# Last batch, chunks two by two: seven products for eight in every second block of a and b

## The chip, the cores and the metric

The kernel runs on one core of one Trainium2 chip. The metric is device time of one execution in microseconds (us); the time before the change is the median of three runs. Engines are named as the profile names them: PE is TensorE (matmuls), PEld its weight loads, DVE is VectorE, ACT is ScalarE, POOL is GpSimd, SP is SyncE, which here only issues DMAs. Every engine works through its own instructions in order, and waits on semaphores for the others.

## The reference

Four batches, N = 5824 tokens, C = 256 channels, d_ff = 1024. A cross-covariance attention gives for each batch a 256 x 256 matrix, and a multiplicative feed-forward follows:

```python
qn = q / (norm(q, axis=1) + 1e-06); kn = k / (norm(k, axis=1) + 1e-06)
s = kn.transpose(0, 2, 1) @ qn / tau
a = softmax(s)                     # [B, 256, 256]
x = (v @ a).reshape(B * N, 256)
out = ((x @ w1) * (x @ w2) @ w3) @ w_out
```

## The kernel before, in words

**Folding.** Since v @ a @ w1 = v @ (a @ w1), the kernel folds the attention matrix into w1 and w2 once per batch: `Wf[n]` holds, for each half `ct` of the channels, a 128 x 1024 block for a (w = 0) and one for b (w = 1). `fold` (L439) runs eight PSUM tiles of 128 x 512 through `fold_mm` (L420); four of them are scaled by the softmax sums on ACT (L435) and four on DVE (L437). Likewise w3 @ w_out is one 1024 x 256 matrix `W_sb`. The folds of batch n run near the end of batch n - 1.

**Main loop.** The 5824 tokens of a batch are 11 chunks of 512 (c = 0 to 10) and one of 192 (c = 11). `emit_ab` (L651) is one slot: for chunk c and block j (128 of the 1024 hidden channels, j = 0 to 7) it issues two 128x512 matmuls into a PSUM tile for a, two for b (L657, one for each channel half `ct`), an ACT copy of a to SBUF as bf16 (L663) and the DVE product a*b (L676) into `abh`, which lies in the pool "big". The tiles for a and b rotate over four PSUM banks, ab0 to ab3. The other four banks are out0, out1, out2 and G.

**Seven products.** With all eight blocks of a chunk there, `seven_products` (L552) does (a*b) @ W_sb, as 2 x 2 blocks, in Strassen and Winograd's form: seven products of eight 128x128 matmuls (L570) in place of eight, in seven or eight groups. It needs four sums S1 to S4 of halves of `abh` (L589 and L592, 128x1024 bf16), made on POOL in batches 0 to 2 and on DVE in the last batch, and sums of W_sb (`comb_T`), made once. S2 is made from S1, S4 from S2. Four products go one after another through PSUM tile A, and after each an ACT copy `keep` (L580) takes the running sum out before the next may be added to it; B and C are joined by DVE adds (L583). In the last batch the sums stand inside the groups: S1 at once, S2 and p1, S3 and p5, p6, S4 and p7, p2, p4, p3. In the other batches each sum is issued two slots after the one before it. The last full chunk (c = 10) and the short one go through `emit_out` (L719).

**Order of the work.** It is written out by hand. For each slot the loop (L972) runs what an agenda holds for the modelled clock (loads, transposes, the softmax of the next batch), then `emit_ab`, then takes groups from `pend` as long as `room` (2, which is one group of a product or two of `emit_out`) lasts, then the sums that are due. So a typical slot is a, b and one product. A load is preceded by `gate` (L642), a one-element POOL copy that waits for the newest `abh` and so holds the DMA issue behind it (L120).

Of the kernel before, what the change touches and what calls it, by code (L numbers as in the profile page):

```python
# [9 lines left out]
AF = mybir.ActivationFunctionType  # L10
ALU = mybir.AluOpType
F32 = DT.float32
BF16 = DT.bfloat16

P = 128
# [3 lines left out]
LAG_FAST = 4  # L19
BIG_BUFS = 21  # L20
MM_COL = 1.0 / 2400.0
MM_FIX = 0.0025
# [3 lines left out]
def kernel(  # L26
# [12 lines left out]
    nc = tc.nc  # L39

    B, N, C = q.shape
    T, D = out.shape
    F = moe_w1.shape[1]
# [205 lines left out]
    S = {}  # L249
# [27 lines left out]
    def soft_units(n):  # L277
# [142 lines left out]
        def fold_mm(key, c2, tag="ab", on_act=True):  # L420

            w, c1, lo, hi = key
            if c2 == 0:
                turn = (lo // 512 * 4 + w * CT + c1) % 3
                home = bank(tag) if n == 0 or turn == 2 else {"tag": ("out2", "G")[turn], "bufs": 1}
                st[key] = psum.tile([P, 512], F32, name=f"fold_{n}_{w}_{c1}_{lo}", **home)
            m = st[key][:, : hi - lo]
            nc.tensor.matmul(  # L428
                m, lhsT=st["e"][:, c2, c1 * P : (c1 + 1) * P], rhs=w12[:, c2, w, lo:hi],
                start=(c2 == 0), stop=(c2 == CT - 1),  # L430
            )
            if c2 == CT - 1:
                dst = Wf[n][:, c1, w, lo:hi]
                if on_act:
                    nc.scalar.activation(out=dst, in_=m, func=AF.Copy, scale=st["rs"][:, c1 : c1 + 1])  # L435
                else:
                    nc.vector.tensor_scalar_mul(dst, m, st["rs"][:, c1 : c1 + 1])  # L437

        def fold(i, tag="ab"):  # L439
            h, rest = divmod(i, 4)  # L440
            w, c1 = divmod(rest, 2)
            for c2 in range(CT):
                fold_mm((w, c1, h * 512, (h + 1) * 512), c2, tag, i % 2 == 0 or (n == 0 and i == 7))

# [42 lines left out]
            + [(0.43, 16.5 + 1.1 * i, lambda i=i: fold(i)) for i in range(8)]  # L487
        )


    clock = [0.0]
    agenda = []

    def run_due(upto=None):
        lim = clock[0] if upto is None else upto
        while agenda and agenda[0][0] <= lim:
            _, _, cost, fn = agenda.pop(0)
            clock[0] += cost
            fn()
# [3 lines left out]
    def at(t, cost, fn):  # L503
        seq[0] += 1
        agenda.append((t, seq[0], cost, fn))
# [9 lines left out]
    def rhs_of(b, c, ct):  # L515
        vT, vTt = vTs[b]
        if c < NCH - 1:
            return vT[:, 4 * c : 4 * c + 4, ct, :]
        return vTt[:, ct, :]
# [32 lines left out]
    def seven_products(b, c, k1, k2):  # L552

        T = comb["T"]
        a11, a21 = k1[:, :, : 2 * P], k1[:, :, 2 * P :]
        a12, a22 = k2[:, :, : 2 * P], k2[:, :, 2 * P :]
        w1 = [W_sb[:, j, :P] for j in range(4)]
        w21 = [W_sb[:, 4 + j, :P] for j in range(4)]
        w22 = [W_sb[:, 4 + j, P:] for j in range(4)]
        t1, t2, t3, t4 = ([T[:, i, j, :] for j in range(4)] for i in range(4))  # L560
        st, sums = {}, {}
        tags = {"A": "out0", "B": "out1", "C": "out1" if b < B - 1 else "out2"}
        adder = nc.gpsimd if b < B - 1 else nc.vector

        def product(nm, a, w, first=False):
            if first:
                st[nm] = psum.tile([P, 2, P], F32, tag=tags[nm], name=f"prod{nm}_{b}_{c}", bufs=1)
            for j in range(4):
                for i in range(2):
                    nc.tensor.matmul(  # L570
                        st[nm][:, i, :], lhsT=a[:, j, i * P : (i + 1) * P], rhs=w[j],
                        start=(first and j == 0 and i == 0), stop=(j == 3), skip_group_check=True,
                    )
            clock[0] += 8 * (P * MM_COL + MM_FIX)

        def quarter(r, d):
            return st["o"][:, 2 * r : 2 * r + 2, d * P : (d + 1) * P]

        def keep(r, d):
            nc.scalar.copy(quarter(r, d), st["A"])  # L580

        def join(nm, r, d):
            nc.vector.tensor_add(quarter(r, d), st[nm], quarter(r, d))  # L583

        def operand(i):

            x = sums[i] = work.tile([P, 4, 2 * P], BF16, tag=f"S{i}", name=f"S{i}_{b}_{c}", bufs=1)
            if i == 1:
                adder.tensor_add(x, a21, a22)  # L589
            else:  # L590
                u, w = {2: (sums.get(1), a11), 3: (a11, a21), 4: (a12, sums.get(2))}[i]
                adder.tensor_sub(x, u, w)  # L592

        def p1():
            st["o"] = work.tile([P, 4, D], F32, tag="o_sb", name=f"osb_{b}_{c}", bufs=3)
            product("A", a11, w1, True)
            keep(0, 0)

        def p5():
            product("C", sums[1], t1, True)  # L600

        def p6():
            product("A", sums[2], t2)
            keep(0, 1)

        def p7():
            product("A", sums[3], t3)
            keep(1, 1)

        def p2():  # L610
            product("B", a12, w21, True)

        def p4():
            product("A", a22, t4)
            keep(1, 0)

        def p3():
            product("C", sums[4], w22)

        def store():  # L620
            rows = out[b * N : b * N + NT * P, :].rearrange("(p i) c -> p i c", i=NT)
            nc.sync.dma_start(out=rows[:, 4 * c : 4 * c + 4, :], in_=st["o"])

        def S(i):
            return lambda: operand(i)

        def J(*x):
            return lambda: join(*x)

        def then(fn):  # L630
            return lambda: following.append(fn)

        if b == B - 1:
            return [S(1)], [
                [S(2), p1], [S(3), p5], [p6], [S(4), p7], [J("C", 1, 1), p2],
                [J("B", 0, 0), p4], [p3, J("C", 0, 1), store],
            ]
        return [S(1), S(2), S(3), S(4)], [
            [p1], [p2, then(J("B", 0, 0))], [p6], [p5], [p7], [then(J("C", 1, 1))], [p4], [p3, then(J("C", 0, 1)), then(store)],
        ]  # L640
# [10 lines left out]
    def emit_ab(b, c, j):  # L651
# [27 lines left out]
        if not seven(b, c):  # L679
            if b == B - 1 or c == NCH - 1:  # L680
                lag = LAG if b == B - 1 else FT + LAG_FAST
                pend.append((slot[0] + lag, 1, lambda only=None: emit_out(b, c, j, ab, only)))
            elif j == FT - 1:
                for i in range(FT):
                    fn = lambda i=i, ab2=tuple(halves[c]): emit_half(b, c, i, ab2)
                    pend.append((slot[0] + 1 + LAG_FAST + i, 1, fn))
        elif j == FT - 1:
            sums, groups = seven_products(b, c, *halves[c])
            for i, fn in enumerate(sums):
                due_sums.append((slot[0] + 2 * i, fn))  # L690
            ready = slot[0] + 1 + (LAG_FAST if b < B - 1 else 0)
            for i, group in enumerate(groups):
                wait = 0 if b == B - 1 else i
                pend.append((ready + wait, 2, lambda group=group: [fn() for fn in group]))
        clock[0] += 4 * (n * MM_COL + MM_FIX)

    def emit_half(b, c, i, ab2):

# [212 lines left out]
    def make_agenda(b):  # L911
# [34 lines left out]
        if b == 0:  # L946
            for i in range(4):
                at(COMB + 2.6 * i, 0.0, lambda i=i: combine_weights(i))
        if n == B:
            agenda.sort()  # L950
            return
# [14 lines left out]

    for b in range(B):
        make_agenda(b)
        order = [(c, j) for c in range(NCH) for j in range(FT)]
        if b == 0:  # L970
            order[: 2 * FT] = [(c, h * 4 + j) for h in range(2) for c in range(2) for j in range(4)]
        for s, (c, j) in enumerate(order):  # L972
            run_due()
            while following:
                following.pop(0)()
            scores_due(s)
            emit_ab(b, c, j)
            lag = 0
            if b == B - 1 and c >= NCH - 2:
                lag = LAG_END if c == NCH - 1 else LAG + (LAG_END - LAG) * (j + 1) // FT  # L980
            room = 2
            while slot[0] > W_SLOT and len(pend) > lag and pend[0][0] <= slot[0] and pend[0][1] <= room:
                _, size, fn = pend.pop(0)
                fn()
                room -= size
                run_due()
            while due_sums and due_sums[0][0] <= slot[0]:
                due_sums.pop(0)[1]()
        run_due(1e9)
# [39 lines left out]
```

## Time and profile before

| What | Value |
|---|---|
| Time of the program, median of 3 runs | 555.21 us (555.05 to 555.32) |
| Span of the profiled execution, first to last instruction | 553.5 us |
| PE, DVE, ACT, POOL busy over the span | 542.1, 435.5, 375.8, 304.8 us |
| Last batch: from its first 128x512 matmul to its last | 431.8 to 541.2 us |
| PE busy from 441.75 to 541.20 us | 99.45 of 99.45 us |
| DVE, ACT, POOL busy in the same stretch | 86.33, 60.98, 2.94 us |
| One 128x512 bf16 sum on POOL | not in the program; 128x1024: 2.13 us |

The profile shows one execution, so sums of durations are to be set against its span of 553.5 us; the median of the runs is 1.7 us above it, which covers what lies outside the first and the last instruction. A recorded duration of a DVE or ACT instruction can overlap the next one a little, so the rate of an engine is read from the distance of starts. The recorded end of a matmul is modelled.

### The profile page before, as it was taken

To read this page: it belongs to the slowest core of one execution; us is meant where nothing else is said; L and a number is where in the kernel's file an instruction comes from. 1 tells how busy PE (TensorE), PEld (TensorE's weight loads), DVE (VectorE), ACT (ScalarE), POOL (GpSimd) and SP (SyncE) were. 2 spreads that over 40 slices of the span, in tenths; PEclk is the share of its full clock that TensorE was granted. 3 is DMA by queue.
4 is the path that set the end of the run, shared out by engine and by line. 5 is a ranking of instruction groups with operands and counts; after the bars stand their busy time and mean duration, and the time that the engine had idled before them with its cause. 6 is when DMAs were issued, how large, how long until landed. Compare 5 with 4: busy or idle time off the path is not lost.

```text
span 553.5 us, 12330 instructions
## 1 busy us (share of the span) xinstructions
PE 542.1 (98%) x4630; PEld 352.9 (64%) x4630; DVE 435.5 (79%) x789; ACT 375.8 (68%) x757; POOL 304.8 (55%) x257
## 2 busy tenths in 40 slices
PE   7799999999999999999999999999999999999997
PEld 4564577766666666666667566666666666666665
DVE  5567747899976787988876788888877688988984
ACT  5436647788866777777766777777766666566663
POOL 4150022678889678889887588898987400010000
PEclk9999999999999999999999999999999999999999
DMA  9999888975666879576554777875650245343102
GB/s 213 211 206 209 167 164 201 224 180 82 152 140 155 191 150 165 126 147 136 128 127 122 153 153 156 164 147 124 147 115 40 83 117 117 91 110 82 77 40 97
DMA packets 74972, 77.61 MB, mean 140 GB/s; under 512 B 54176, under 2 KB 58784, under 8 KB 74912
## 3 DMA queue, kind: packets, MB, share of 16 engines
q0 software_dynamic: 15616, 38.93, 40.3%
q1 hardware_dynamic: 58928, 37.17, 24.2%
q8 instruction: 36, 0.59, 0.4%
q10 hardware_dynamic: 368, 0.72, 0.3%
q14 instruction: 24, 0.20, 0.1%
HBM read 78.91 MB, written 23.86 MB: 186 GB/s over the span
## 4 chain that ended last, share of the span: by engine, by line
PE 93%; DMA 5%; DVE 0%; ACT 0%; POOL 0%; issue 0%; POOLq 0%
PE a L657 28%; PE b L657 28%; PE prodA L570 13%; PE prodC L570 6%; PE G L200 5%; PE prodB L570 3%; DMA k<-in_k_dram 3%; PE o L707 3%; PE fold L428 2%; DMA q<-in_q_dram 2%; PE o_out L738 2%; PE w L882 1%; PE G L271 0%; PE narrow L452 0%; PE sqq L259 0%
## 5 line engine op out<-in xcount | busy, mean ns | idle before, releaser
L676 DVE TENSOR_TENSOR abh<-as,b 128x512 bf16<-128x512 bf16 x352 | 240.0, 684 | 82.0 <-ACT as L663 76.2
L663 ACT CAST as<-a 128x512 bf16<-128x512 f32 (+1 forms) x384 | 215.4, 562 | 94.8 <-PE a L657 61.5
L657 PE MATMUL a<-vT,Wf 128*128 128x512 bf16 x704 | 209.4, 379 | 0.1
L657 PE MATMUL b<-vT,Wf 128*128 128x512 bf16 x704 | 209.4, 379 | 0.0
L657 PEld LDWEIGHTS <-Wf 128*128 128x128 bf16 x1536 | 141.1, 98 | 100.6 <-issue 0.8
L570 PEld LDWEIGHTS <-S 128*128 128x128 bf16 x1248 | 82.6, 98 | 34.3
L212 DVE TENSOR_TENSOR acc<-acc,sq 128x512 f32<-128x512 f32 x132 | 91.6, 694 | 3.0 <-ACT sq L197 1.9
L580 ACT COPY osb<-prodA 128x256 f32<-128x256 f32 x156 | 58.1, 372 | 42.0 <-PE prodA L570 41.4
L589 POOL TENSOR_TENSOR S<-abh,abh 128x1024 bf16<-128x1024 bf16 x29 | 61.7, 2127 | 32.1 <-DVE abh L676 16.6
L570 PEld LDWEIGHTS <-abh 128*128 128x128 bf16 x936 | 62.0, 98 | 25.7 <-issue 0.2
L592 POOL TENSOR_TENSOR S<-S,abh 128x1024 bf16<-128x1024 bf16 x29 | 61.8, 2131 | 1.9
L592 POOL TENSOR_TENSOR S<-abh 128x1024 bf16<-128x1024 bf16 x29 | 61.8, 2131 | 0.1
L592 POOL TENSOR_TENSOR S<-abh,S 128x1024 bf16<-128x1024 bf16 x29 | 61.7, 2129 | 0.1
L645 POOL COPY gate_t<-abh 1x1 bf16<-1x1 bf16 x39 | 7.2, 185 | 80.1 <-DVE abh L676 79.9
L570 PE MATMUL prodA<-comb_T,S 128*128 128x128 bf16 x624 | 47.6, 219 | 0.0
L200 PE MATMUL G<-k,q 128*128 128x256 bf16 x276 | 47.0, 273 | 0.0
L197 ACT ACTIVATE sq<-q 128x512 f32<-128x512 bf16 x69 | 43.8, 634 | 0.0
L197 ACT ACTIVATE sq<-k 128x512 f32<-128x512 bf16 x69 | 43.4, 628 | 0.0
L583 DVE TENSOR_TENSOR osb<-prodC,osb 128x256 f32<-128x256 f32 x78 | 32.5, 417 | 0.0
L200 PEld LDWEIGHTS <-q 128*128 128x128 bf16 x276 | 23.9, 98 | 3.6
L570 PE MATMUL prodB<-W_sb,abh 128*128 128x128 bf16 x312 | 23.8, 219 | 0.1
L570 PE MATMUL prodC<-comb_T,S 128*128 128x128 bf16 x312 | 23.8, 219 | 0.0
(139 smaller groups left out, 444.0 us busy)
## 6 DMA issues: line engine op xcount, KB each, us to landing
out_dram<-osb SPq DMA_DIRECT2D x44, 512.0 KB, 3.2
k<-in_k_dram POOLq DMA_DIRECT2D x19, 512.0 KB, 8.3
v<-in_v_dram POOLq DMA_DIRECT2D x19, 512.0 KB, 5.2
q<-in_q_dram POOLq DMA_DIRECT2D x18, 512.0 KB, 5.8
w_wout<-in_moe_w_dram POOLq DMA_DIRECT2D x1, 2048.0 KB, 21.6
k<-in_k_dram POOLq DMA_DIRECT2D x4, 320.0 KB, 6.5
v<-in_v_dram POOLq DMA_DIRECT2D x4, 320.0 KB, 5.4
q<-in_q_dram POOLq DMA_DIRECT2D x3, 320.0 KB, 5.2
```

The lines of the kernel that those rows point to most:

```text
L197: nc.scalar.activation(out=sqs[0][:, :, part, :], in_=src[:, o : o + 2, :], func=AF.Square)
L200: nc.tensor.matmul(G[:, ct, :], lhsT=qt[:, i, ct * P : (ct + 1) * P], rhs=kt[:, i, :], start=(pr == 0 and part == 0 and ct == 0), stop=(pr ...
L212: nc.vector.tensor_add(accs[n], accs[n], sqs[0][:, part - 2])
L570: nc.tensor.matmul(st[nm][:, i, :], lhsT=a[:, j, i * P : (i + 1) * P], rhs=w[j], start=(first and j == 0 and i == 0), stop=(j == 3), skip_ ...
L580: nc.scalar.copy(quarter(r, d), st["A"])
L583: nc.vector.tensor_add(quarter(r, d), st[nm], quarter(r, d))
L589: adder.tensor_add(x, a21, a22)
L592: adder.tensor_sub(x, u, w)
L657: nc.tensor.matmul(t[:, :n], lhsT=Wf[b][:, ct, w, j * P : (j + 1) * P], rhs=rhs_of(b, c, ct), start=(ct == 0), stop=(ct == CT - 1),)
L663: nc.scalar.copy(a_sb[:, :n], tiles[0][:, :n])
L676: nc.vector.tensor_mul(ab, a_sb, tiles[1])
L707: nc.tensor.matmul(t[:, k, :], lhsT=ab2[j // 4][:, j % 4, (2 * h + k) * P : (2 * h + k + 1) * P], rhs=W_sb[:, j, :], start=(j == 0 and k = ...
```

## The change

Only the work for batch 3, the last, is changed. Its chunks 0 to 7 go in pairs (0,1), (2,3), (4,5), (6,7). A pair has 16 slots, k = 0 to 3 with four steps `sub` each. Block 2k+1 of both chunks is done as before, with eight 128x512 matmuls (`plain`). Block 2k of both chunks is one 2 x 2 product, of the two channel halves of the weights of a and b with the two chunks' two channel halves, and is done with seven 128x512 matmuls in place of eight. For that:

- `weight_sums` makes four sums of the folded weights (128 x 1024 each, S[0] to S[3] in `wsums`) by eight `scalar_tensor_tensor` instructions on DVE that read the fold's PSUM tile; for this batch ACT scales all eight folds, and the folds of b come before those of a.
- `token_sum` makes four sums per pair of `v` transposed (128x512 bf16 each, T[0] to T[3] in `tsums`) on POOL, during the pair before.
- In `emit_pair` the partial sums lie in PSUM tiles X, Y, T and Z, which are read while they are still being added to: ACT copies X to Y (PSUM to PSUM) and T to SBUF (`t5`, float32); DVE adds X and `t5` into Z (PSUM) and into `b1` (bf16); then four DVE products write `abh`.
- The sums S1 to S4 of chunks 0 to 6 go back to POOL, those of chunk 7 stay on DVE, and both are issued two slots apart, as in the other batches. The products of both chunks of a pair start only after the pair's 16 slots, the second chunk's eight slots after the first's. From chunk 8 on `room` is 4: two product groups may go into one slot. Chunks 8 and 9 keep the sums inside the groups.

The core of the diff:

```diff
-                turn = (lo // 512 * 4 + w * CT + c1) % 3
+                turn = (lo // 512 * 4 + ((1 - w) if n in PAIRED else w) * CT + c1) % 3
...
-                if on_act:
+                if n in PAIRED:
+                    nc.scalar.activation(out=dst, in_=m, func=AF.Copy, scale=st["rs"][:, c1 : c1 + 1])
+                    weight_sums(w, c1, lo, hi, m)
...
+        def weight_sums(w, c1, lo, hi, m):
...
+            S = [wsums[n][x // 2][:, x % 2, lo:hi] for x in range(4)]
+            b1 = Wf[n][:, 0, 1, lo:hi]
+            todo = {
+                (1, 0): [], (1, 1): [(0, b1, ALU.add)], (0, 0): [(1, S[0], ALU.subtract), (2, b1, ALU.subtract)],
+                (0, 1): [(3, S[1], ALU.add)],
+            }
+            for x, other, op in todo[w, c1]:
+                nc.vector.scalar_tensor_tensor(
+                    out=S[x], in0=m, scalar=st["rs"][:, c1 : c1 + 1], in1=other, op0=ALU.mult, op1=op
...
+    def token_sum(b, c, i):
+        if i == 0:
+            tsums[b, c] = in_pool.tile([P, 4, 4, P], BF16, tag="big", name=f"tsum_{b}_{c}", bufs=BIG_BUFS)
+        t = tsums[b, c]
+        b11, b12, b21, b22 = (rhs_of(b, c + d, ct) for ct in range(CT) for d in range(2))
+        if i == 0:
+            nc.gpsimd.tensor_sub(t[:, 0], b12, b11)
+        elif i == 1:
+            nc.gpsimd.tensor_sub(t[:, 1], t[:, 0], b22)
+        elif i == 2:
+            nc.gpsimd.tensor_sub(t[:, 2], b22, b12)
+        else:
+            nc.gpsimd.tensor_add(t[:, 3], b21, t[:, 1])
...
+        late = b == B - 1 and c >= 2 + max(PAIRED[b])
-        adder = nc.gpsimd if b < B - 1 else nc.vector
+        adder = nc.vector if b == B - 1 and c > max(PAIRED[b]) else nc.gpsimd
...
+    def queue_products(b, c, delay=0):
+        sums, groups = seven_products(b, c, *halves[c])
+        late = len(sums) == 1
+        if late:
+            pend.append((slot[0], 0, sums[0]))
+        for i, fn in enumerate(() if late else sums):
+            due_sums.append((slot[0] + delay + 2 * i, fn))
+        ready = slot[0] + delay + 1 + (0 if late else LAG_FAST)
+        for i, group in enumerate(groups):
+            pend.append((ready + (0 if late else i), 2, lambda group=group: [fn() for fn in group]))
...
+    def pair_begin(b, c, k):
+        x = periods[0] % 2
+        periods[0] += 1
+        st = pairs[b, c, k] = {"x": x}
+        st["X"] = psum.tile([P, 512], F32, name=f"X_{b}_{c}_{k}", tag=f"ab{x}", bufs=1)
+        j = slice(2 * k * P, (2 * k + 1) * P)
+        mm512(st["X"], Wf[b][:, 0, 0, j], rhs_of(b, c, 0), True)
+        st["Y"] = psum.tile([P, 512], F32, name=f"Y_{b}_{c}_{k}", tag="G", bufs=1)
+        nc.scalar.copy(st["Y"], st["X"])
...
+        if sub == 0:
+            st["T"] = psum.tile([P, 512], F32, name=f"T_{b}_{c}_{k}", tag="ab2", bufs=1)
+            mm512(st["T"], S[0][:, js], T[:, 0], True)
+            st["t5"] = work.tile([P, 512], F32, tag="sq", name=f"t5_{b}_{c}_{k}", bufs=2)
+            nc.scalar.copy(st["t5"], st["T"])
+            a = plain(b, c, jn, 0, "ab3")
+            st["a"] = cast(a, f"as_{b}_{c}_{jn}")
+        elif sub == 1:
+            mm512(X, S[1][:, js], T[:, 1], False)
+            st["Z"] = psum.tile([P, 512], F32, name=f"Z_{b}_{c}_{k}", tag="ab2", bufs=1)
+            nc.vector.tensor_add(st["Z"], X, st["t5"])
+            t = plain(b, c, jn, 1, f"ab{1 - st['x']}")
+            nc.vector.tensor_mul(ab(0, jn), st["a"], t)
+            last_ab[0] = ab(0, jn)
+            mm512(st["Y"], W[:, 1, 0, js], rhs_of(b, c, 1), False)
+            st["a0"] = cast(st["Y"], f"as_{b}_{c}_{jw}")
+        elif sub == 2:
+            a = plain(b, c + 1, jn, 0, "ab3")
+            st["a"] = cast(a, f"as_{b}_{c + 1}_{jn}")
+            mm512(X, S[2][:, js], T[:, 2], False)
+            st["b1"] = work.tile([P, 512], BF16, tag="b_sb", name=f"bs_{b}_{c + 1}_{jw}", bufs=1)
+            nc.vector.tensor_add(st["b1"], X, st["t5"])
+            mm512(st["Z"], S[3][:, js], rhs_of(b, c + 1, 1), False)
+        else:
+            nc.vector.tensor_mul(ab(1, jw), st["b1"], st["Z"])
+            t = plain(b, c + 1, jn, 1, "G")
+            nc.vector.tensor_mul(ab(1, jn), st["a"], t)
+            def end():
+                mm512(X, W[:, 1, 1, js], T[:, 3], False)
+                if k < 3:
+                    pair_begin(b, c, k + 1)
+                elif c + 2 in PAIRED[b]:
+                    pair_begin(b, c + 2, 0)
+                nc.vector.tensor_mul(ab(0, jw), st["a0"], X)
+                last_ab[0] = ab(0, jw)
+                if k == 3:
+                    queue_products(b, c)
+                    queue_products(b, c + 1, FT)
...
+            late = emit_pair(b, c, j, *sub) if sub else emit_ab(b, c, j)
+            if sub and c + 2 in PAIRED[b] and sub[0] == 3:
+                token_sum(b, c + 2, j)
...
-            room = 2
+            room = 4 if b == B - 1 and not sub else 2
```

`plain` issues the two matmuls of a or b into the bank named, and `cast` is the ACT copy to bf16 (L663 before). In PSUM, X lies in ab0 and ab1 in turn, and b of block 2k+1 of the first chunk in the other of the two; T and Z lie in ab2, a of block 2k+1 in ab3; Y and b of block 2k+1 of the second chunk in G. The program has 16 matmuls fewer.

## The prediction

> **What bounds the kernel now.** I read the page's busy shares and slices first, then the chain that ended last, then the windows of the last batch, then its timeline.
>
> ```profile
> PE 542.1 (98%) x4630; PEld 352.9 (64%) x4630; DVE 435.5 (79%) x789; ACT 375.8 (68%) x757; POOL 304.8 (55%) x257
> ...
> PE   7799999999999999999999999999999999999997
> ...
> POOL 4150022678889678889887588898987400010000
> ...
> PE 93%; DMA 5%; DVE 0%; ACT 0%; POOL 0%; issue 0%; POOLq 0%
> ```
>
> PE is the bound: busy in every slice but the first two and the last, and 93% of the chain. POOL is empty in the last nine slices, which is the last batch. The windows (us, then busy us of PE, PEld, DVE, ACT, POOL; clock, DMA):
>
> ```profile
> 441.75:541.20 99.45, 99.45 (x879) 62.31 (x878) 86.33 (x149) 60.98 (x120) 2.94 (x7) 1.00 0.35 89
> ```
>
> So in the last batch each removed matmul is worth its full time, and any wait of PE costs its full time: there is no idle PE to hide it in. One slot, from the timeline:
>
> ```profile
> 537.81 0.59 PE L657 MATMUL a<-vT,Wf 128*128 128x512 bf16 x2
> 538.24 0.59 PE L657 MATMUL b<-vT,Wf 128*128 128x512 bf16 x2
> 538.44 0.58 ACT L663 CAST as<-a 128x512 bf16<-128x512 f32 x1 [0.72 <-DVE abh L676]
> 538.67 0.61 PE L570 MATMUL prodA<-comb_T,abh 128*128 128x128 bf16 x8
> 539.12 0.59 PE L657 MATMUL a<-vT,Wf 128*128 128x512 bf16 x2
> 539.32 0.37 ACT L580 COPY osb<-prodA 128x256 f32<-128x256 f32 x1 [0.29 <-PE prodA L570]
> ```
>
> (The columns are start, duration, engine, line, operation, count, and in brackets the idle time before and what ended it.)
>
> Starts give the rates: two 128x512 matmuls in 0.43 us (0.217 each, called m), a product of eight in 0.45. ACT starts 0.63 after the first a matmul, so 0.41 after the second: a 128x512 result reaches another engine 0.41 us after its matmul starts. A keep starts 0.65 after its product does.
>
> **Rows for the new work.**
>
> ```profile
> 330.28 1.42 DVE L212 TENSOR_TENSOR acc<-acc,sq 128x512 f32<-128x512 f32 x2
> ...
> 331.57 0.58 ACT L663 CAST as<-a 128x512 bf16<-128x512 f32 x1
> 332.03 0.64 ACT L197 ACTIVATE sq<-k 128x512 f32<-128x512 bf16 x1
> ...
> 331.61 1.27 DVE L676 TENSOR_TENSOR abh<-as,b 128x512 bf16<-128x512 bf16 x2
> ...
> 463.38 0.58 ACT L663 CAST as<-a 128x512 bf16<-128x512 f32 x1 [0.72 <-DVE abh L676]
> ...
> 464.00 0.69 DVE L676 TENSOR_TENSOR abh<-as,b 128x512 bf16<-128x512 bf16 x1 [0.29 <-ACT as L663]
> ...
> 417.42 2.12 POOL L592 TENSOR_TENSOR S<-abh 128x1024 bf16<-128x1024 bf16 x1
> 419.50 2.12 POOL L592 TENSOR_TENSOR S<-abh,S 128x1024 bf16<-128x1024 bf16 x1
> ```
>
> DVE 128x512 with one PSUM input: 0.68 long; two independent ones take 1.27, so 0.59 to 0.60 from start to start; two where the second reads the first's result take 1.42, so 0.73. ACT 128x512: 0.58 long, 0.46 from start to start. From engine to engine 0.04: ACT ends at 463.96, the DVE product that it feeds starts at 464.00. POOL: 2.09 per 128x1024 sum, 2.2 after a sum it reads.
>
> **1. Removed: 16 matmuls.** 16 x 0.217 = **-3.5 us**, all on the path.
>
> **2. A loop through DVE and ACT.** Per k the change adds two DVE adds (6 instructions for 4) and one ACT copy (5 for 4), and chains them. Y lies in bank G after b of the second chunk, so the ACT copy of X to Y (start y) waits for the DVE product that reads that b. From y, with no product in between:
> - ACT copies T from y+0.46, done y+1.05. The second X matmul waits until Y is copied: y+0.64.
> - DVE adds Z at y+1.09, multiplies at 1.69.
> - PE does b, b, Y, a, a (a waits for ACT's copy of the last a, until 1.55) and the third X at 1.99, which reaches DVE at 2.40, where b1 starts. b1*Z reads b1: 2.40 + 0.73 = 3.13. The product that reads G: 3.73, done 4.42.
> - Next y: **4.46**. PE has 15 m = 3.25 us of work for that k.
>
> With a product between the two X's the third X reaches DVE 0.45 later, y+2.80, and b1 starts then: loop 2.80 + 0.73 + 0.60 + 0.73 = 4.86. In a k without one there, DVE's own queue decides (two instructions and a join of 0.34 after Z, b1 at 2.63): 4.69. PE's work in those k is 15 m + 4 x 0.45 = 5.04 and 15 m + 3 x 0.45 = 4.59. They alternate, 9.55 against 9.63 for two: PE is just the bound, and I cost the loop at nothing where products are dense. The cover is thin: 0.1 us more in the loop costs about 1 us over the eleven k.
>
> Where products are missing the loop is the bound. They now begin only at k = 1 of pair (2,3). k = 0 of the first pair still has those of batch 2; k = 1 and 2 have the short chunk's single matmuls (0.11 each; one between the X's makes the loop 4.57), k = 3 and the next k = 0 have nothing. Four loops, 4.57 + 4.57 + 4.46 + 4.46 = 18.1, stand against PE work between the same X matmuls of 3.69 + 3.58 + 3.25 + 3.70 = 14.2 (15 m each, four and three singles, none, one product). At the start of k = 1 another 0.4 is lost: y comes 1.1 + 0.41 + 3.6 after k = 0's T, X 0.64 later at 5.75, PE is there at 5.35. Together 3.9 + 0.4 = **+4.3 us**. Before, products began after one chunk and PE was full here. The ACT copy from PSUM to PSUM has no row; bounds 0.37 and 0.69 (L580, 256 wide, and L435, which also scales); eight hand-offs of 0 to 0.1: loop 4.1 to 5.1, cost 2.5 to 6.5. I take 0.58, since L663 and L713 read PSUM and differ only in where they write.
>
> **3. POOL in pairs (2,3) to (6,7).** It gets 8 sums per pair back, 6 x 2.09 + 2 x 2.2 = 16.9, four token sums, and a load with its gate and gaps, 1.0. A 128x512 sum has no row: bounds are the one-element copy (L645, 0.185) and 128x1024 (2.13); half the elements give 1.07 without a fixed part and 1.16 with one of 0.185; I take 1.1. 16.9 + 4.4 + 1.0 = **22.3 us** per pair. PE needs 60 m + 14 x 0.45 = 19.3. All of PE stands behind a product that waits for its sum. From the first S1, 0.6 after the y that opens pair (2,3), POOL runs without a gap to S2 of chunk 4: 0.6 + 2 x 22.3 + 4.4 = 49.6. PE wants that S2 for p6 at k = 1 of pair (6,7): 7.3 (T of k = 1 at 3.87, when ab2 is read; X at 5.1; then 3 m, p2, 4 m) + 2 x 19.3 = 45.9. PE waits 3.7; two DMA issues of the next load (1.7) before the second chunk's S2 add 0.5. **+4.2 us**, in p6 and p7. With token sums of 0.6: nothing; of 2.13: 8 x 1.0 more, +12.
> The loads of v ride in the same queue up to 5 us late. They land 5.2 and, transposed, 4.3 later, and are used 18 us after: hidden; if not, a token sum waits and all behind it. SP issues the same stores a chunk later; they take 3.2 us of the 10 between them and nothing on the path waits for one. The token sums of pair (0,1) go between chunk 8's sums in batch 2: S3 ends at 410.3 and is used at 413.2, S4 412.4 and 416.6, so 2 and 3 x 1.1 fit. Nothing; 1 us if a token sum takes 1.5.
>
> **4. The folds.** ACT gets 4 x 0.69 more; DVE 8 sums for 4 scalings (L437, 0.745, the nearest row: PSUM in, one scalar), +3.0. From 418 to 428 DVE is busy 6.85 and ACT 6.53 of 10: it becomes 9.9 and 9.3. It just fits in their idle time, but banks are held longer: 0 to 1, I take 0.2.
>
> **5. The tail.** The backlog of products is a chunk and a half longer, so chunk 8's go two to a slot beside chunk 10, and chunk 9's beside the short chunk, where a and b take 0.34. There p7 comes directly after p6 into tile A and waits for the keep: 0.65 + 0.37 + 0.04 after p6's start, PE being free after 0.45: 0.6. Sums made on DVE just before their use (S1 0.60, S2 0.73 behind a product of 0.60): p6 and p7 of chunk 8 0.2 each, p6 of chunk 9 0.4. The short chunk's output waits for a bank 0.25 more. **+1.6 us** (0.5 to 3); before, PE waited for none of this.
>
> **Sum.** -3.5 + 4.3 + 4.2 + 0.2 + 1.6 = +6.8 us on 553.5, a span of 560.3. The median is 1.7 above the span: **562.0 us**, 1.2% slower.
>
> The Trainium skill has a rule against the change at one more place ("SBUF — State Buffer", section "Who interferes with whom"): a VectorE instruction with two SBUF inputs and a GpSimd instruction that reads SBUF shut each other out for a whole instruction. The sums of chunk 7 on DVE meet those of chunk 6 on POOL; by the rule a DVE sum could wait up to 2.1 us there. In the trace before, DVE made such sums only while POOL was idle, so no row shows it; by the rule the sum would be up to 2 us larger, without it it stands.
>
> **Rivals.**
> - *POOL keeps up* (token sums 0.6 or less): 555.2 - 3.5 + 4.3 + 0.2 + 1.6 = 557.8. For it: strided 128-element runs have no row. Against: the 2.09 per 1024 elements repeats 29 times a line. 0.2.
> - *The waits are covered, faster*: the loop is 0.8 shorter than worked out (copies quicker, hand-offs hidden), and POOL keeps up: 555.2 - 3.5 + 0.5 to 1.5 = 552.2 to 553.2. The price decides at a loop of 3.6 us, the PE work of those k. For it: DVE has 13% and ACT 39% idle in the window. Against: latency, not load, fills the loop. 0.13.
> - *POOL is worse*: token sums near 128x1024's 2.13: 568 to 574. 0.07.
> - *Gain and waits cancel*: loop 4.1, POOL stall 1, small tail: about 555. The change not doing what it says, for instance matmuls removed but PE at the old end for another chain, comes out here too. 0.08.
> - *The forecast*, loop and POOL both: 0.52, own range 559 to 566.
>
> Range 555.0 to 567.0: it leaves out the faster case and the worst one, 0.20 together. Under 0.2% (1.1 us) a measurement of this kernel can't tell a change from none. Faster 0.13, same 0.08, slower 0.79.
>
> **What would show it.** Right: PE idle by 0.8 to 1.2 us per k in k = 1 to 3 of the first pair and k = 0 of the second, ended by ACT's copy of X or a DVE add; PE waits for POOL's S2 and S3 in p6 and p7 of chunks 1 to 4; POOL without a gap there; token sums of about 1.1; 16 matmuls fewer; an end later by about 7. Wrong: PE full from 432 to 540 (parts 2 and 3), token sums far from 1.1 (part 3), or waits of PE in the folds longer than 1 us (part 4).

## The result, and the profile after

The changed kernel takes **564.52 us** (median of 4 runs, 564.39 to 564.67), the kernel before beside it 555.24: 1.0168 times the time, 95% interval 1.0154 to 1.0183. It is slower by 9.3 us, inside the range given, 2.5 above the 562.0 forecast. The profiled execution has a span of 562.4 us, 8.9 more than before.

Busy times, PE's and POOL's slices, and the chain by engine, from the page of the changed kernel:

```profile
PE 544.6 (97%) x4614; PEld 351.0 (62%) x4614; DVE 439.9 (78%) x797; ACT 382.6 (68%) x777; POOL 381.0 (68%) x301
...
PE   7799999999999999999999999999999899999996
...
POOL 4250023588887798889876688889899279999200
...
PE 84%; POOL 5%; DMA 5%; DVE 3%; ACT 1%; issue 1%; DVEq 0%; ACTq 0%; POOLq 0%
```

The 16 matmuls are gone (4630 to 4614), and PE still looks full: one slice of 8. What changed is the chain: PE had 93% of it and now has 84; POOL has 5 and DVE 3, which had nothing. The same shows in the last batch's window (99.45 us long, columns as in the window of before):

```profile
441.75:541.20 99.45, 94.71 (x773) 55.25 (x772) 81.81 (x140) 61.56 (x126) 74.04 (x48) 1.00 0.34 80
```

PE is busy for 94.7 of 99.45 us where it had no idle time.

Start times of PE in the two timelines give the account in us. Every row but the first is the time by which PE came late against its own work:

| part | forecast | measured | from, in the changed kernel |
|---|---|---|---|
| 16 matmuls removed | -3.5 | -3.5 | 16 x 0.217 |
| folds | +0.2 | +1.7 | batch 3's first X at 433.49; its first a was at 431.81 |
| loop, k without products | +4.3 | +4.9 | 433.49 to 457.73 is 24.2; PE's work there 19.3 |
| loop, dense k | 0 | +1.1 | two k take 4.94 + 4.90; PE's work is 9.64: 0.1 in each of eleven k |
| POOL | +4.2 | +2.1 | three k of 5.50, 5.42, 5.87 in place of 4.9 |
| tail | +1.6 | +2.5 | first a of chunk 8, at 513.27, to the end; 0.2 of it the kernel before has too |
| sum | +6.8 | +8.8 | span +8.9 |

**The loop.** PE, DVE and ACT in k = 2 of the first pair, from the timeline (some lines left out):

```profile
443.81 0.57 ACT L759 COPY Y<-X 128x512 f32<-128x512 f32 x1 [1.75 <-DVE abh L817]
...
444.44 0.38 PE L747 MATMUL X<-tsum,wsum 128*128 128x512 bf16 x1 [0.34 <-ACT Y L759]
...
444.92 0.70 DVE L801 TENSOR_TENSOR Z<-X,t 128x512 f32<-128x512 f32 x1 [0.60 <-ACT t L795]
...
445.86 0.38 PE L747 MATMUL X<-tsum,wsum 128*128 128x512 bf16 x1
...
446.27 0.69 DVE L812 TENSOR_TENSOR bs<-X,t 128x512 bf16<-128x512 f32 x1
...
447.10 0.69 DVE L815 TENSOR_TENSOR abh<-bs,Z 128x512 bf16<-128x512 bf16 x1
...
447.70 0.68 DVE L817 TENSOR_TENSOR abh<-as,b 128x512 bf16<-128x512 bf16 x1
...
448.47 0.57 ACT L759 COPY Y<-X 128x512 f32<-128x512 f32 x1 [0.96 <-DVE abh L817]
```

Read it as a ring: ACT's copy of X, which waited for the DVE product (L817); PE's second X (444.44), which waited for the copy; the matmuls behind it in PE's queue up to the third X (445.86); DVE's b1 0.41 after that, b1*Z and the product; the next copy 4.66 later. Z (444.92), which waited for ACT's copy of T, is done well before b1 and doesn't lengthen the ring. The copy from PSUM to PSUM takes 0.57. The starts of this copy, subtracted, are the length of each k, and are used below for every kernel: 5.29, 4.62, 4.66, 4.63, 4.62, then 4.94, 4.85, 4.95, 4.90, 4.94, 5.50, 5.42, 5.87, 4.94, 4.91. The ring holds in the first five, POOL adds to three, and the rest, called dense (three or four products each), take 4.9. The last k of the last pair has no next copy, which leaves fifteen lengths for sixteen k.

**POOL.** All three waits of PE for it that stand as a line of their own, from PE's timeline:

```profile
483.19 0.62 PE L610 MATMUL prodA<-comb_T,S 128*128 128x128 bf16 x8 [0.48 <-POOL S L632]
491.26 0.62 PE L610 MATMUL prodA<-comb_T,S 128*128 128x128 bf16 x8 [0.50 <-POOL S L632]
494.43 0.62 PE L610 MATMUL prodA<-comb_T,S 128*128 128x128 bf16 x8 [0.60 <-POOL S L632]
```

They stand before p7 of chunk 2 and p6 and p7 of chunk 3, and each ends 0.05 or 0.06 after POOL's sum for that product. A token sum takes 1.15 (1.1 was taken) and POOL needs 21.9 us per pair (22.3).

**Tail.** DVE just before PE's longest wait there, and that wait, from the timeline:

```profile
538.68 0.69 DVE L629 TENSOR_TENSOR S<-abh,abh 128x1024 bf16<-128x1024 bf16 x1
539.40 0.69 DVE L632 TENSOR_TENSOR S<-S,abh 128x1024 bf16<-128x1024 bf16 x1
540.01 0.42 DVE L623 TENSOR_TENSOR osb<-prodC,osb 128x256 f32<-128x256 f32 x1
...
540.48 0.61 PE L610 MATMUL prodC<-comb_T,S 128*128 128x128 bf16 x8 [0.87 <-DVE osb L623]
```

p5 of chunk 8 goes into the bank that chunk 7's last join must first empty, and that join stands in DVE's queue behind S1 and S2 of chunk 8.

### The profile page after: what moved, and what is told of

Its sections match the earlier page's. It is cut to its first block, busy times and chain, and to the rows that moved or that the text cites. A ratio compares the mean times of both kernels' runs of the same rounds, so it can differ in the third digit from the quotient of the medians.

```text
span 562.4 us, 12358 instructions
## 1 busy us (share of the span) xinstructions
PE 544.6 (97%) x4614; PEld 351.0 (62%) x4614; DVE 439.9 (78%) x797; ACT 382.6 (68%) x777; POOL 381.0 (68%) x301
## 4 chain that ended last, share of the span: by engine, by line
PE 84%; POOL 5%; DMA 5%; DVE 3%; ACT 1%; issue 1%; DVEq 0%; ACTq 0%; POOLq 0%
PE a L697 23%; PE b L697 22%; PE prodA L610 11%; PE G L200 5%; PE prodC L610 5%; POOL S L632 3%; PE prodB L610 3%; DMA k<-in_k_dram 3%; PE o L845 2%; PE fold L428 2%; DMA q<-in_q_dram 2%; PE X L747 2%; PE o_out L876 2%; PE b L747 2%; PE a L747 1%; PE w L1020 1%
## 5 line engine op out<-in xcount | busy, mean ns | idle before, releaser
L716 DVE TENSOR_TENSOR abh<-as,b 128x512 bf16<-128x512 bf16 x288 | 196.3, 684 | 71.8 <-ACT as L703 66.0
L703 ACT CAST as<-a 128x512 bf16<-128x512 f32 (+1 forms) x320 | 178.1, 559 | 72.7 <-PE a L697 53.8
L697 PEld LDWEIGHTS <-Wf 128*128 128x128 bf16 x1280 | 118.2, 98 | 85.3 <-issue 2.1
L697 PE MATMUL a<-vT,Wf 128*128 128x512 bf16 x576 | 171.3, 379 | 0.1
L697 PE MATMUL b<-vT,Wf 128*128 128x512 bf16 x576 | 171.3, 379 | 0.1
L629 POOL TENSOR_TENSOR S<-abh,abh 128x1024 bf16<-128x1024 bf16 x36 | 76.6, 2127 | 36.1 <-PE prodC L610 13.2
L632 POOL TENSOR_TENSOR S<-S,abh 128x1024 bf16<-128x1024 bf16 x36 | 76.7, 2130 | 2.3
L632 POOL TENSOR_TENSOR S<-abh 128x1024 bf16<-128x1024 bf16 x36 | 76.7, 2131 | 0.1
L632 POOL TENSOR_TENSOR S<-abh,S 128x1024 bf16<-128x1024 bf16 x36 | 76.7, 2130 | 0.1
L747 PEld LDWEIGHTS <-Wf 128*128 128x128 bf16 x176 | 15.8, 97 | 16.4 <-issue 5.5
L610 PE MATMUL prodC<-comb_T,S 128*128 128x128 bf16 x312 | 23.8, 219 | 0.9 <-DVE osb L623 0.9
```

What stands on the lines that cost most here:

```text
L610: nc.tensor.matmul(st[nm][:, i, :], lhsT=a[:, j, i * P : (i + 1) * P], rhs=w[j], start=(first and j == 0 and i == 0), stop=(j == 3), skip_ ...
L697: nc.tensor.matmul(t[:, :n], lhsT=Wf[b][:, ct, w, j * P : (j + 1) * P], rhs=rhs_of(b, c, ct), start=(ct == 0), stop=(ct == CT - 1),)
L703: nc.scalar.copy(a_sb[:, :n], tiles[0][:, :n])
L716: nc.vector.tensor_mul(ab, a_sb, tiles[1])
L747: nc.tensor.matmul(dst, lhsT=lhsT, rhs=rhs, start=start, stop=True, skip_group_check=True)
```

## The experiments

Theory: four separate waits (folds, loop, POOL's queue, tail) cost more than the products are worth. Rivals: POOL alone does it; DVE's load (not the latency of a ring) does it. Each kernel was timed against the kernel before on the same chip, which stood at 555.0 to 555.2; so a difference between two rows of the table can be off by 0.2 us, and where that matters the text gives the difference to the kernel before.

| run | median us | ratio to before, 95% |
|---|---|---|
| the change | 564.5 | 1.0154 to 1.0183 |
| e1 POOL without later token sums | 562.0 | 1.0109 to 1.0136 |
| e2 folds of the change alone | 556.8 | 1.0019 to 1.0040 |
| e3 G freed first | 569.0 | 1.0236 to 1.0264 |
| e4 first two chunks plain | 560.8 | 1.0089 to 1.0120 |
| e5 other banks | 570.4 | 1.0262 to 1.0290 |
| e6 products held back | 563.0 | 1.0131 to 1.0158 |
| e7 chunk 8's sums on POOL | 563.0 | 1.0131 to 1.0158 |
| e8 weight sums from SBUF | 572.6 | 1.0302 to 1.0330 |
| f1, f2, f3 cures together | 561.3, 561.6, 560.9 | 1.0090 to 1.0140 |
| g1 all cures, three pairs | 557.2 | 1.0023 to 1.0050 |

**e1: POOL without the later token sums**

```diff
-            if sub and c + 2 in PAIRED[b] and sub[0] == 3:
-                token_sum(b, c + 2, j)
-        W, T = Wf[b], tsums[b, c]
+        W, T = Wf[b], tsums[b, 0]
```

> Edit: the token sums are made for the first pair only, and the later pairs multiply by those of the first (12 GpSimd sums of 1.15 us left out; the output of chunks 2 to 7 of the last batch is not the reference's). All else is the changed kernel, 564.5 us. Theory (POOL's queue is one of four causes): POOL needs 21.9 - 4.6 = 17.3 us per pair against PE's 19.3, so PE's waits for S2 and S3 go and 3.2 us come back: 561.3 us. Rival A (POOL hides a loop through DVE and ACT that is as long): the loop of 4.62 measured where products are missing grows to 4.8 and 5.0 where they are dense, against 5.04 and 4.59 of PE, so about 1 of the 3.2 us is lost again: 562.3. Rival B (POOL alone is the cause of the slowdown): 555 or below.

562.0, 2.5 us less. POOL is out of the chain (0%). The k that were 5.50, 5.42 and 5.87 are dense ones; two lines of ACT's timeline:

```profile
482.11 0.57 ACT L759 COPY Y<-X 128x512 f32<-128x512 f32 x1 [1.14 <-PE T L747]
487.00 0.57 ACT L759 COPY Y<-X 128x512 f32<-128x512 f32 x1 [1.40 <-DVE abh L817]
```

They are 4.89 apart, and 4.95 in the next k: 9.84 for two against PE's 9.64. The second still waits for the DVE product; the first waits for PE. So rival A holds beside the theory: POOL cost 2.1 (by the k) to 2.5 (by the times), and behind it the ring costs 0.1 us per dense k. Rival B falls: without POOL's part the kernel is still 6.8 us slower than before.

**e2: the folds alone**, in the kernel before: `fold_mm`, `fold` and `weight_sums` of the change, and nothing else of it.

> Edit: the kernel before (555.2 us) with only the folds of the change: the last batch's eight foldings are all scaled on ACT, in the change's order, and DVE makes the eight 128x512 weight sums from PSUM; nothing reads the sums, and the last batch is computed as before. Theory (the sums hold banks and push DVE's queue): PE stands 1.8 us in the folds as it does in the changed kernel: 557.0. Rival (the stall in the folds comes from what the change does elsewhere, such as the first pair's token sums on POOL): 555.4.

556.8: 1.7 us more than before, as the theory has it. The wait is the same one as in the changed kernel; PE's timeline of e2:

```profile
428.43 0.33 PE L680 MATMUL b<-vTt,Wf 128*128 128x192 bf16 x2 [0.93 <-DVE left L691]
```

The b of the short chunk needs a bank that a DVE product must read first, and that product stands behind three weight sums. This wait is 0.93 of the 1.7; the rest is made of gaps of 0.14 to 0.28 between PE's starts. e2 keeps ACT's four added scalings and DVE's sums together, so it doesn't show which of the two makes those. DVE's timeline of the changed kernel, where the same wait ends at 428.68:

```profile
426.10 0.75 DVE L455 SCALAR_TENSOR_TENSOR wsum<-fold,rs,Wf 128x512 bf16<-128x512 f32 x1
426.95 0.75 DVE L455 SCALAR_TENSOR_TENSOR wsum<-fold,rs,wsum 128x512 bf16<-128x512 f32 x1
427.62 0.74 DVE L455 SCALAR_TENSOR_TENSOR wsum<-fold,rs,Wf 128x512 bf16<-128x512 f32 x1
428.28 0.34 DVE L708 TENSOR_TENSOR left<-as,b 128x192 bf16<-128x192 bf16 x1
```

**e3: two DVE instructions change places**

```diff
-            nc.vector.tensor_mul(ab(1, jw), st["b1"], st["Z"])
             t = plain(b, c + 1, jn, 1, "G")
             nc.vector.tensor_mul(ab(1, jn), st["a"], t)
+            nc.vector.tensor_mul(ab(1, jw), st["b1"], st["Z"])
```

> Edit: in the fourth part of each k the product that reads bank G is put ahead of b1*Z on DVE; two instructions change places, nothing else does. Theory (the loop from ACT's copy into G, over Z, b1 and the product that reads G, sets the pace where products are missing): G is free 0.6 to 0.7 us earlier, but bank ab2 0.6 later, so the loop falls from 4.63 to the way through ab2: T to t5 0.41, t5 to Z 0.63, Z to the third X 0.7, to b1 0.41, to the product of G 0.6, to b1*Z 0.6, its 0.68 and 0.04: 4.1. Four k by 0.5: -2.0 us, 562.5. Rival (DVE's load, which is the same, sets the pace): 564.5, no change. Second rival (the wait moves to ab2, and T is as late as Y was): 564 to 565, with PE waiting at T in place of X.

569.0, 4.5 us more, above all three expectations; the second rival had the place right (PE waits at T) and the price wrong. The lengths of k: 4.81, 4.70, 4.77, 4.43, 4.44, then 5.78 and 5.31 in turn. In the k with nothing else the ring did get shorter (4.43 for 4.63; 4.1 expected). In the dense k PE now stands at T, and the timeline shows why: its bank is freed by b1*Z, now 0.6 later.

```profile
467.91 0.68 DVE L817 TENSOR_TENSOR abh<-bs,Z 128x512 bf16<-128x512 bf16 x1
...
468.64 0.38 PE L747 MATMUL T<-tsum,wsum 128*128 128x512 bf16 x1 [0.55 <-DVE abh L817]
```

DVE has the same instructions, and the time moved by 4.5 us: order and latency set the pace, not DVE's load. Its rival falls; the theory of the place (G alone) falls with it, for the dense k. In these two orders the ring closes through the bank that is freed last: G in the change, ab2 here.

**e4: chunks 0 and 1 plain**, three pairs, token sums of pair (2,3) during chunk 0:

```diff
-    PAIRED = {B - 1: (0, 2, 4, 6)}
+    PAIRED = {B - 1: (2, 4, 6)}
...
```

> Edit: chunks 0 and 1 of the last batch are computed as before, three pairs remain (12 products fewer for 16), and the token sums of pair (2,3) are made during chunk 0. Theory: of the four causes two go. The loop without products (4.9) goes, as products start in chunk 1 and each k of pair (2,3) has them; POOL starts its sums a chunk earlier and has 47 us of work to the S2 that PE wants 55 us later, so its 3.2 go; 0.9 of the gain goes too. 564.5 - 4.9 - 3.2 + 0.9 = 557.3, if the loop costs nothing where products are dense, and to 558.5 if it is 0.1 us per k longer than PE's work. Rival (the loop's cost comes with every pair, through DVE's load): only a fourth of the slowdown goes: 561.5 to 562.5.

560.8, 3.7 us less than the change where 6 to 7 were expected. POOL's wait went as forecast (it has 0% of the chain). The loop's did not: k takes 5.51, 4.95, 4.89, **4.63, 4.66**, then 4.9. Products of a pair become ready only at its end, both chunks at once, and those of chunk 1 run out in k = 2 of the first pair. So wherever the first pair stands, it ends in k without products. The expectation's step that failed is "each k of pair (2,3) has them".

**e5: G read by no DVE product** (the edit shortened; the second X and Z leave sub 1 for sub 0)

```diff
         if sub == 0: (T, t5)
+            mm512(X, S[1][:, js], T[:, 1], False)
+            ... Z = X + t5
             a = plain(b, c, jn, 0, "ab3")
         sub 2:
-            a = plain(b, c + 1, jn, 0, "ab3")    (ahead of X and Z)
+            a = plain(b, c + 1, jn, 0, "G")      (behind X and Z)
         sub 3:
-            t = plain(b, c + 1, jn, 1, "G")
+            t = plain(b, c + 1, jn, 1, "ab3")
```

> Edit: the b of a pair's second chunk goes to bank ab3 and the a of the second chunk to G, so that G is last read by an ACT cast early in the k and ACT's copy into G waits for no DVE product; the second X matmul and Z's add go ahead of the first a, and the third X and Z ahead of the second a. The same instructions, DVE's order unchanged. Theory (latency of the loop through G sets the pace of the k without products, DVE's load doesn't): the loop becomes that of DVE alone, b1 to b1*Z 0.73, then 0.6 three times to Z, which then waits for nothing, 0.6 to the product that needs the first a, 0.6 to 0.8 to b1: about 4.1 in place of 4.63, 3 x 0.5 in the first pair and the 0.4 at its start: -1.9 us, 562.6. In the later pairs nothing is gained, as POOL sets the pace there from its first sum on. Rival (DVE's load sets the pace): 564.5.

570.4, 5.8 us more. The two k with nothing else fell to 4.30; dense k rose to 5.64 and 5.68. PE's timeline, in a dense k:

```profile
463.59 0.38 PE L747 MATMUL X<-tsum,wsum 128*128 128x512 bf16 x1 [0.50 <-ACT Y L759]
463.81 0.59 PE L747 MATMUL a<-vT,Wf 128*128 128x512 bf16 x2
```

PE takes its instructions in the order of the program: the a behind the waiting X starts 0.22 after it. In the change two a matmuls and a product stand between T and the second X and cover ACT's copies; here nothing does, and PE waits 0.5 in each. The expectation saw only the DVE side of the ring. It also took POOL for the bound of the later pairs, which it is in three k only.

**e6: products of batch 2's chunk 10 held back by eight slots**

```diff
+        hold_back = 8 if (b, c) == (B - 2, NCH - 2) else 0
-        ready = slot[0] + delay + 1 + (0 if late else LAG_FAST)
+        ready = slot[0] + delay + 1 + (0 if late else LAG_FAST) + hold_back
```

> Edit: the products of chunk 10 of the batch before the last are held back by eight slots; four that stood in the folds and three of the first k now stand in k = 1 and 2 of pair (0,1), and the short chunk's single matmuls in k = 3. Theory (the loop of k without products costs what PE has too little of): four products leave the path, 4 x 0.45 = 1.8, k = 0 falls from 5.3 to 4.6, k = 1 and 2 rise from 4.6 to 4.9: -1.9 us, 562.6. Rival A (the pace there is set by DVE's load or by the pair itself, products or not): the products come on top in their new place, 564.5. Rival B (in the folds the products cover the stall): their place stands idle, 564.5, with PE idle before the first X in place of later.

563.0: set against the kernel before on its own chip, 1.3 us less than the change (1.9 expected). k takes 4.61, 4.95, 4.90, 4.71, 4.62 for 5.29, 4.62, 4.66, 4.63, 4.62: the sum is the same (23.8) with more of PE's work inside, and the first X comes 1.3 earlier. Two copies, from ACT's timeline, with seven products in these two k where there were none:

```profile
437.20 0.57 ACT L760 COPY Y<-X 128x512 f32<-128x512 f32 x1 [1.79 <-DVE abh L818]
442.15 0.57 ACT L760 COPY Y<-X 128x512 f32<-128x512 f32 x1 [1.14 <-PE T L748]
447.05 0.57 ACT L760 COPY Y<-X 128x512 f32<-128x512 f32 x1 [1.40 <-DVE abh L818]
```

Seven products are 3.1 us of PE, and the two k grew by 0.6: four fifths of what stands in such a k is free. Rivals A and B fall.

**e7: chunk 8's sums on POOL**

```diff
+        early = b == B - 1 and c == 2 + max(PAIRED[b])
-        adder = nc.vector if b == B - 1 and c > max(PAIRED[b]) else nc.gpsimd
+        adder = nc.vector if b == B - 1 and c > max(PAIRED[b]) and not early else nc.gpsimd
...
```

> Edit: chunk 8's four sums are made on POOL, which is idle from 524 us on, in place of DVE just before their use; products in the same order. Theory (p5 of chunk 8 waits 1.04 because the join that frees its bank stands behind two sums on DVE): that wait goes, and some of the 0.6 at chunk 9's p5 and p6: 563.2 to 563.5. Rival (the wait is that of the join itself, which follows its product): p5 waits as before, 564.5; or worse where POOL's sums (2.13 each, 8.5 from 528 on) are late for p6: 565.

563.0: set against the kernel before on its own chip, 1.3 us less than the change. p5 of chunk 8 starts with its bank free, 0.43 after the b matmuls ahead of it, where it started 1.47 after them:

```profile
538.76 0.59 PE L702 MATMUL b<-vT,Wf 128*128 128x512 bf16 x2
539.19 0.61 PE L611 MATMUL prodC<-comb_T,S 128*128 128x128 bf16 x8
```

So the tail's largest wait was the join behind two sums. The waits at chunk 9's p6 and p7 (0.25 and 0.46) stayed.

**e8: weight sums from SBUF**

```diff
-                nc.vector.scalar_tensor_tensor(
-                    out=S[x], in0=m, scalar=st["rs"][:, c1 : c1 + 1], in1=other, op0=ALU.mult, op1=op
-                )
+                nc.vector.tensor_tensor(out=S[x], in0=Wf[n][:, c1, w, lo:hi], in1=other, op=op)
```

> Edit: the eight weight sums read ACT's scaled result in SBUF (bf16) in place of the bank with a scaling of their own; order and engine are kept. Theory (the sums hold the banks of the folds and cost DVE 0.75 each): a 128x512 sum of two SBUF operands takes about 0.4, no bank waits for it, and most of the 1.8 us in the folds goes: 562.8 to 563.3. Rival (the Trainium skill, SBUF, Who interferes with whom: a VectorE instruction with two SBUF inputs and GpSimd's reads shut each other out): POOL is busy nine tenths of that time with sums of 2.13, so a DVE sum can take up to 2 us and holds the products of the short chunk behind it: 565 or more.

572.6, 8.1 us more. DVE and POOL in e8's timeline, and the two waits of PE (columns start, duration):

```profile
422.72 2.31 POOL L630 TENSOR_TENSOR S<-abh,S 128x1024 bf16<-128x1024 bf16 x1
...
423.16 2.15 DVE L455 TENSOR_TENSOR wsum<-Wf,wsum 128x512 bf16<-128x512 bf16 x1
...
425.23 0.41 DVE L455 TENSOR_TENSOR wsum<-Wf 128x512 bf16<-128x512 bf16 x1
...
426.03 1.01 PE L608 MATMUL prodC<-comb_T,S 128*128 128x128 bf16 x8 [2.04 <-DVE osb L621]
...
426.50 0.41 DVE L455 TENSOR_TENSOR wsum<-Wf,wsum 128x512 bf16<-128x512 bf16 x1
...
431.99 2.29 POOL L630 TENSOR_TENSOR S<-abh 128x1024 bf16<-128x1024 bf16 x1
...
432.24 2.33 DVE L455 TENSOR_TENSOR wsum<-Wf 128x512 bf16<-128x512 bf16 x1
...
434.88 0.48 PE L695 MATMUL b<-vTt,Wf 128*128 128x192 bf16 x2 [4.03 <-DVE left L706]
```

The same sum takes 0.41 while POOL is idle (425.03 to 427.65) and 2.15 or 2.33 while POOL makes a sum; each of the five slow ones ends 0.28 or 0.29 after the POOL sum beside it, as it would if it had to wait for that one's end. POOL's own grow from 2.12 to 2.31. That is what the Trainium skill says ("SBUF — State Buffer", section "Who interferes with whom"): a VectorE instruction with two SBUF inputs and a GpSimd instruction that reads SBUF lock each other out. The change's own sums read PSUM and took 0.74 to 0.75 beside the same POOL sums, as the same section says of an instruction with one SBUF input. The 8.1 us are not all waiting: PE stands 2.04 and 4.03 us behind the slow sums, and after each of these pauses its clock is halved for some microseconds (last section).

**f1, f2, f3: cures together.** e7's edit; chunk 3 by eight products, to relieve POOL; and more products held back (f3: chunk 10 by eight slots; f1: chunk 9 by six too; f2: by eight and ten).

> Edits together, the whole reference computed: chunk 8's sums on POOL (measured -1.5); chunk 3 of the last batch by eight products, so that POOL has 8.45 us less in pair (4,5), for 0.34 more on PE; the products of chunks 9 and 10 of the batch before held back by six and eight slots, so that seven and more of them stand in pair (0,1). Theory (four separate causes, so their cures add): -1.5; -2.5 + 0.3 for POOL; with the filling, k = 0 to 2 as dense as later ones (4.9), three more products off the path than with chunk 10 alone: -1.5 - 1.0; the folds one to a slot: -0.5 to -1. Together 564.5 - 6.7 = 557.8, to 557.3. Rival (the waits stand in for each other, curing one shows the next): half of it, 561.

> As the one before, with chunks 9 and 10 held back by eight and ten slots: all but three of their 14 products and the short chunk's singles stand in pair (0,1) and the first k of the next, which leaves no k without. Theory: of the loop's 4.9 us four fifths are covered, -3.9, if the folds and the short chunk, now nearly without products, don't become bound by ACT and DVE: 564.5 - 1.5 - 2.2 - 3.9 - 0.7 = 556.2. Rival (ACT and DVE bound the folds when PE has less there: a slot has 1.35 us of DVE and 1.27 of ACT against 1.30 of PE): what is gained in the pair is lost in the folds, 558 to 559.

> As the first of the three, with only chunk 10 held back (by eight, measured alone -1.5): the check of the sum. Theory: 564.5 - 1.5 (tail) - 2.2 (POOL) - 1.5 = 559.3. Rival (the cures don't add): 561 to 562.

561.3, 561.6 and 560.9: f3 came 1.6 above its sum (1.2 if the two cures in it are taken at 1.3 each), f1 and f2 3.5 to 4.0 and 5.4 above theirs. The rivals' times (561 for f1, 561 to 562 for f3) are the nearer ones: the cures don't add. In f3 POOL's cure gave 1.1 in place of 2.2: p7 of chunk 2 still waited for its sum (k of 5.48), and the eight-product chunk made one k 5.27. Chunk 3 was the wrong one to relieve. In f1 and f2 most filled k took 4.9 to 5.05, as in e6 (f1's first 5.88: PE waits 0.51 for a bank that a product of the short chunk frees), but the folds lost what the pair gained: f1's PE waits 0.99 and 0.19 behind weight sums and 0.66 behind a join. f2's rival puts that down to ACT and DVE being full there. They aren't: from 415 to 432 f2's DVE is busy for 13.2 of 17 us and ACT for 11.4. By what ends PE's waits there (weight sums, a product, a join), it is again the order in DVE's queue.

**g1: all cures, three pairs.** Chunks 0 and 1 plain; folds as before the change; weight sums on POOL from SBUF during chunk 0; the 14 products of chunks 0 and 1 three to a k; e7's edit.

> Edits together, the whole reference computed: chunks 0 and 1 plain, three pairs (12 products fewer); the folds as before the change, and the weight sums made on POOL from SBUF during chunk 0, four of 128x1024 (2.13 each), the token sums of pair (2,3) behind them; the 14 products of chunks 0 and 1 spread three to a k over the five k that had none or would run dry; chunk 8's sums on POOL. Theory (the removed products are worth what they are, and all that the change lost are the four waits): -2.6 for the products; folds 0; POOL 0; about 0.1 to 0.2 per k over twelve k for the loop, +1.2 to 2.4; 0.9 of the tail and 0.4 at the first k's start left: 555.0 + 0.0 to 1.1 = 555.0 to 556.1, about the kernel before. Rival A (some cause isn't among the four): 558 or more. Rival B (the loop costs nothing where three or four products stand in each k): 553.8.

557.2: between the theory and rival A, 0.37% slower than before (interval 0.23 to 0.50). The folds' wait is gone (batch 3's first a at 431.44; 431.81 before), and POOL has 0% of the chain. What is left is the ring and the tail: the five filled k take 5.77, 4.63, 5.26, 4.63 and 4.82, 25.1 against 22.5 of PE's work; the six after them 29.5 against 28.9; PE's starts at chunk 9's p5, p6 and p7 come 0.2, 0.4 and 0.6 late; and the first X 0.3. These make 4.7 against the 2.6 that the products give back: 2.1, and 2.0 were measured. Of all versions with the change's products this is the fastest; none beats the kernel before.

## Why the prediction was right, and where it was not

The mechanisms held: four new waits, each larger than nothing and together larger than the products. The sizes were off by 2 us in sum, and the sum flatters them: POOL came 2.1 below its forecast and hid half of the 4.1 that the folds, the two parts of the loop and the tail came above theirs. That these errors had different signs was luck.

- **Part 1, removed products:** 16 matmuls less, as counted. Their worth was not measured alone; the account closes to 0.1 us with it, and so does g1's with its twelve.
- **Part 2, loop without products:** 4.9 for 4.3. The ring was 4.62 to 4.66 where I had 4.46 to 4.57: DVE to ACT takes 0.09 (0.04 was taken for every hand-off) and b1 to b1*Z 0.83 in the lines above (0.73). e3 and e5, which change the order and not the work, and e6, which fills it, show that latency and order set it and not DVE's load.
- **Part 2, dense k "costed at nothing":** failed by 1.1. PE was "just the bound, 9.55 against 9.63"; two such k measure 9.84 with POOL out of the way (e1). The text said the cover is thin, 0.1 us more in the loop costing about 1 us; that is what came.
- **Part 3, POOL:** 2.1 for 4.2, mis-sized twice. POOL needs 21.9 per pair, not 22.3; and I set it against PE's 19.3, while a dense pair takes 19.7 for the ring's sake. Both work twice over two pairs: 0.8 + 0.8. POOL can be late only against what PE really does, so two bounds in one place don't add. The remaining 0.5 is what I had put down to two DMA issues ahead of a second chunk's S2; POOL's timeline has one there (0.57, at 466.56 and at 488.47).
- **Part 4, folds:** the step that failed most, 0.2 for 1.7. I compared load with idle time ("9.9 and 9.3 of 10. It just fits"). It fitted: in ten us from 418, 420 or 422 on, DVE is busy for 7.8 to 9.0 us and ACT for 7.2 to 8.3. Load that fits in a window still makes queues: three sums ahead of a product of 0.34 that frees a bank hold PE for 0.93. e2 shows the 1.7 without the rest of the change; how the other 0.7 splits between ACT and DVE stays open. My own sign that part 4 is wrong, more than 1 us of waits in the folds, came.
- **Part 5, tail:** 2.5 for 1.6. Of the waits I named, those at chunk 9's p6 and p7 came (0.4 and 0.6 by PE's starts); chunk 8's p6 and p7 didn't wait. One I had not: the join of chunk 7 behind S1 and S2 of chunk 8, 0.9 to 1.0, which e7 took away.

The rule on shared reads, left out of the sum, cost nothing in the change: POOL's last sum ends at 524.17, and DVE's first of chunk 7 begins at 524.09 and takes 0.69. e8 shows the rule at work, and at what price. One reading was loose: in the last nine slices before, POOL has a 4 and a 1 and not zeros only, which changes nothing.

## What to carry to other kernels

Before trading matmuls for adds on other engines, close the ring on paper: from the copy that frees a bank through every engine to the next such copy, and compare that latency with PE's work in one turn; at 4.6 us of ring and 3.3 us of PE, 0.2 us of matmul less per turn could not pay; where PE had 4.6 to 5.0 us in a turn, the ring took back 0.1 of the 0.2. An engine that has idle time on the average is not free: ask what stands behind the added instruction in its queue, and which bank that one frees. And when several waits sit on one stretch, cure them one at a time: one covers the next (e1), and moving work to fill a hole opens one where it came from (f1, f2).

## What the runs showed of the hardware

- A DVE sum of two SBUF operands, 128x512 bf16: 0.41 us with POOL idle, 1.40 to 2.33 with POOL's sums beside it (e8).
- After a pause of PE of 2.04 us in e8 its granted clock was half. By windows of one us the clock was 1.00 until 426, 0.52, 0.50, 0.50 and 0.78 in the four after, and 1.00 again from 430; eight matmuls of 128x128 that take 0.61 elsewhere took 1.01. In the pause of 4.03 us that ended at 434.88 the clock fell to 0.50 from 433, and it stayed there until 439. In the changed kernel the longest wait is 0.93 in this stretch, and its clock is 1.00 throughout the last batch.
- An ACT copy of 128x512 f32 from PSUM to PSUM takes 0.57, no more than the one to SBUF (0.58).
